# Gated two-branch decode attention on one core: the gate's inputs loaded as three rows and transposed on TensorE, a branch's normalisation on VectorE behind the next unit's scores

## The chip, the core and the metric

The kernel runs on one core of one Trainium2 chip. The core has five engines with instruction queues of their own: TensorE (PE in the profile; its weight loads are PEld), VectorE (DVE), ScalarE (ACT), GpSimd (POOL) and SyncE (SP), which here only issues transfers. An engine works through its own queue in order, and waits at an instruction until the semaphores that it names are there. Transfers between the chip's main memory and the core's buffers run on 16 DMA engines. The metric is the device time of one execution in microseconds (us), lower is better.

## The reference

Two attention branches A and B are computed on the same two tokens `x` (2 x 512) and mixed by a gate. Each branch has its own projection `wq`, its own cached keys and values (2 batches, 32 heads, 4096 positions, 128 numbers each) and its own output projection `wo`. Everything is float32.

```
g = sigmoid((x * gate_w).sum(-1, keepdims=True))
q = (x @ wq)  as 32 heads of 128
p = softmax(q . k_cache * 128 ** -0.5)         # over 4096 positions, for each batch and head
o = p @ v_cache                                # then heads side by side, @ wo
result = g * branch_A + (1 - g) * branch_B     # 2 x 512
```

The caches make nearly all of the bytes: 64 loads of 8.39 MB, beside two of `wq` and two of `wo` of the same size.

## The kernel before

**Units.** The work is cut into 32 units: branch (A, B), batch b (0, 1) and a group g of four heads (0 to 7), in that order, so that units 0 to 15 are branch A and 8, 16 and 24 are the first units of a new batch or branch. `per_branch` is 16, `NU` is 32. A unit loads the keys of four heads as `kt` (128 partitions x 16384 numbers; a partition is one head's run of 128 positions) and the values as `vt` in the same shape.

**One unit.** `scores(u)` multiplies `kt` by the query, which lies in PSUM, in place on VectorE (L147), and sums over the 128 numbers of a head (L149). `soft(u)` takes the maximum on VectorE (L154, L156, L158) and the exponentials on ScalarE (L162, four of them, which also write the sums of the exponentials to `lsum`). `values(u)` multiplies by the values on TensorE (L174). After each second unit ScalarE brings the result to SBUF (L179) and TensorE adds up the four strips into `gat` (L183).

**The end of a batch.** With the last group of a batch `values` calls `outputs(n, b)`: ScalarE copies `gat` (L189), TensorE sums `lsum` over the partitions (L191), VectorE takes the reciprocal of that sum and multiplies it by the gate (L193, L194), TensorE picks each head's row out of `gat` (L197), and ScalarE copies the rows to `rows` with the scale `rl` (L200). With the second batch TensorE also deals the rows out to 128 partitions (L204) and VectorE copies that to `on` (L207). The VectorE instructions L193, L194 and L207 stand in VectorE's queue ahead of the next unit's L147.

**Buffers and the order of the loads.** SyncE issues all large loads in the order in which the program is written, and each waits there until its buffer is free:

- `kt` has two buffers, which are taken in turn by `wq` of A, keys 0, keys 1, and so on; `wq` of B takes one between keys 15 and keys 16, and at the end values 31 and `wo` of B take one each. Keys u+2 can be issued when `scores(u)` has ended. Keys 1 come after `project("A")`, since it reads the buffer that holds `wq` of A (L61).
- `vt` has one buffer. Values u+1 can be issued when `values(u)` has ended (L68). `wo` of A comes last in it.

**The start.** `wq` of A and keys 0 are issued at once by SyncE. The two rows of `x` and `gate_w` are issued by ScalarE as three loads into `xg` (L85 to L88), each of them 128 partitions x 4 numbers, 16 bytes a partition. From `xg` VectorE makes `xb` (L112, the scaled `x`, each number 32 times), `xw` and `zp` (L114, L116); TensorE sums the gate's logit (L119); `project("A")` multiplies `xb` by `wq` on TensorE (L136), 64 matmuls in the program and 128 records in the trace.

**The end.** `bulk` takes the first parts of the output projections on TensorE (L237), a tail of `wo` of B comes in small pieces (L82, L247), and `res` is copied (L250) and stored.

The lines of the program that set the order:

```
    project("A")
    load_k(1)
    load_v(0)
    for u in range(NU):
        scores(u)
        soft(u)
        ...
            load_k(u + 2 if u != per_branch - 1 else per_branch)
        ...
        values(u)
        ...
            load_v(u + 1)
```

Of the kernel before, what the change touches and what calls it, by code (L numbers as in the profile page):

```python
# [8 lines left out]
F32 = mybir.dt.float32  # L9
AF = mybir.ActivationFunctionType  # L10
ALU = mybir.AluOpType
AX = mybir.AxisListType

P = 128
B = 2
H = 32
SK = 4096
DH = 128
D = 512
KC = D // P  # L20
QP = 32
HU = P // QP
SLOTS = SK // QP
VC = 4
# [4 lines left out]
NJ = D * H * DH // (P * D)  # L29
# [8 lines left out]
def tile_gated_decode(ctx: ExitStack, tc: tile.TileContext, ins: dict, out: bass.AP):  # L38
    nc = tc.nc
# [3 lines left out]
    consts = ctx.enter_context(tc.tile_pool(name="consts", bufs=1))  # L43
    work = ctx.enter_context(tc.tile_pool(name="work", bufs=2))
    ps = ctx.enter_context(tc.tile_pool(name="ps", bufs=1, space=bass.MemoryType.PSUM))
# [4 lines left out]
    per_branch = B * HG  # L50
# [31 lines left out]
                nc.sync.dma_start(wo[n][:, i:j], src[:, i:j])  # L82

    load_wq("A")
    xg = consts.tile([P, B + 1, KC], F32)  # L85
    for b in range(B):
        nc.scalar.dma_start(xg[:, b], ins["A_x"][b, 0].rearrange("(p c) -> p c", c=KC))
    nc.scalar.dma_start(xg[:, B], ins["gate_w"].rearrange("(p c) -> p c", c=KC))  # L88
    load_k(0)

    ident = consts.tile([P, P], F32)
    make_identity(nc, ident)
    ones = consts.tile([P, QP], F32)
# [4 lines left out]
    lsum = consts.tile([P, H], F32)  # L98
# [4 lines left out]
    pick = consts.tile([P, VC, H], F32)  # L103
# [3 lines left out]
    deal = consts.tile([H, P + HU], F32)  # L107
    nc.vector.memset(deal, 0.0)
    nc.vector.tensor_copy(deal[:, HU - 1:HU - 1 + P:HU], ident[:H, :H])

    xb = consts.tile([P, B, KC, QP], F32)
    nc.vector.tensor_scalar(xb, xg[:, :B, :, None].to_broadcast([P, B, KC, QP]), SCALE, None, op0=ALU.mult)  # L112
    xw = consts.tile([P, B, KC], F32)
# [6 lines left out]
    gate = consts.tile([H, 4, B], F32)  # L120
# [20 lines left out]
    sc, vp, on = {}, {}, {}  # L141
    gat, rows = {}, {}
# [8 lines left out]
    def soft(u):  # L151
        n, b, g = units[u]
        rm = work.tile([P, QP], F32, name="rm")
        nc.vector.tensor_reduce(rm[:, 0:1], sc[u], axis=AX.X, op=ALU.max)  # L154
        tm = work.tile([P, QP], F32, name="tm")
        nc.vector.transpose(tm, rm[:, 0:1].to_broadcast([P, QP]))  # L156
        nm = work.tile([P, 1], F32, name="nm")
        nc.vector.tensor_reduce(nm, tm, axis=AX.X, op=ALU.max, negate=True)  # L158
        for h in range(HU):
            r = slice(h * QP, (h + 1) * QP)  # L160
            w = pr[r, :, HU:HU + QP].rearrange("p c (a h) -> p c a h", h=HP)[:, :, :, h]
            nc.scalar.activation(w, sc[u][r].rearrange("p (c a) -> p c a", a=VC), AF.Exp, bias=nm[r],  # L162
                                 accum_out=lsum[r, g * HU + h:g * HU + h + 1])
# [23 lines left out]
    def outputs(n, b):  # L187
        gs = work.tile([P, VC, DH], F32, name="vs", bufs=1)
        nc.scalar.activation(gs, gat[n, b].rearrange("p (a d) -> p a d", a=VC), AF.Copy)  # L189
        lt = ps.tile([H, 1], F32, name="small")  # L190
        nc.tensor.matmul(lt, lsum, ones[:, 0:1], start=True, stop=True)  # L191
        rl = work.tile([H, 2], F32, name="rl")
        nc.vector.reciprocal(rl[:, 0:1], lt)  # L193
        nc.vector.tensor_tensor(rl[:, 1:2], rl[:, 0:1], gate[:, 2 + (n == "B"), b:b + 1], op=ALU.mult)  # L194
        o = ps.tile([H, DH], F32, name="small")
        for a in range(VC):
            nc.tensor.matmul(o, pick[:, a], gs[:, a], start=a == 0, stop=a == VC - 1)  # L197
        if b == 0:
            rows[n] = work.tile([H, B, DH], F32, name="rows", bufs=1)
        nc.scalar.activation(rows[n][:, b], o, AF.Copy, scale=rl[:, 1:2])  # L200
        if b == B - 1:
            t = ps.tile([P, B, NJ], F32, name="small")
            for q in range(HU):
                nc.tensor.matmul(t, deal[:, HU - 1 - q:HU - 1 - q + P], rows[n][:, :, q * NJ:(q + 1) * NJ],  # L204
                                 start=q == 0, stop=q == HU - 1)
            on[n] = work.tile([P, NJ, B], F32, name="on")
            nc.vector.tensor_copy(on[n].rearrange("p j b -> p b j"), t)  # L207

    project("A")
    load_k(1)  # L210
# [1 line left out]
    for u in range(NU):  # L212
        scores(u)
        soft(u)
        if u == per_branch - 2:
            load_wq("B")
        elif u == NU - 2:
            load_v(NU - 1)
        elif u == NU - 1:
            load_wo("B")  # L220
        else:
            load_k(u + 2 if u != per_branch - 1 else per_branch)
            if u == per_branch - 1:
                project("B")
                load_k(per_branch + 1)
        values(u)
        if u == NU - 2:
            load_wo("A")
        elif u < NU - 2:
            load_v(u + 1)  # L230

    bulk = ps.tile([P, D], F32, name="q", bufs=4)
    nc.vector.memset(bulk, 0.0)
    for n in "AB":
        for j in range(NJ if n == "A" else NB):
            s = j % STRIPS
            nc.tensor.matmul(bulk[s * QP:s * QP + B], on[n][:, j], wo[n][:, j],  # L237
                             start=n == "A" and j < STRIPS, stop=n == "B" and j >= NB - STRIPS)
# [6 lines left out]
    for j in range(NB, NJ):  # L245
        for s in range(STRIPS):
            nc.tensor.matmul(acc[s * QP:s * QP + B], on["B"][:, j], wo["B"][:, j, s * DH:(s + 1) * DH],  # L247
                             start=False, stop=j == NJ - 1)
# [28 lines left out]
```

## Time and profile before

| what | value |
|---|---|
| time, median of 3 runs | 1368.32 us (1367.85 to 1368.99) |
| time of the profiled execution | 1366.86 us |
| its span, from the first to the last instruction | 1365.1 us |
| VectorE busy | 1127.3 us, 83% of the span |
| TensorE busy (matmuls) | 358.5 us, 26% |
| ScalarE busy | 82.1 us, 6% |
| read from main memory | 570.43 MB, 418 GB/s over the span |

The profiled execution took 1.76 us more than its span, and 1.46 us less than the median of the runs. The profile's times are microseconds from the span's start. A row of the timeline gives the start, the duration, the engine (SPq and ACTq are the queues of SyncE and ScalarE, in which a transfer is issued), the line of the program, the operation, and in square brackets how long the engine had been idle before it and what ended that. A row of the stretches (a window) gives busy times by engine, then the granted TensorE clock, the DMA engines' share and the GB/s; packets count there where they began. A row of the waits gives the total, the number of waits and the longest one.

### The profile page before, as it was taken

How to read it: one execution, taken by the hardware profiler on the slowest of the kernel's cores; microseconds unless marked ns; L12 is line 12 of the kernel's file. 1: busy time of each engine (PE TensorE's matmuls, PEld its weight loads, DVE VectorE, ACT ScalarE, POOL GpSimd, SP SyncE). 2: the span in 40 equal slices, each digit the busy share in tenths (PEclk: the TensorE clock that was granted, in tenths of full speed). 3: DMA queues.
4: the chain of work that ended last, by engine and by line, in shares of the span. 5: the costliest groups of instructions: out<-in, count | busy, mean ns of one | idle time of the engine just before them, and what ended most of it. 6: DMA issues, size and time to landing. Idle time of an engine off the chain costs nothing.

```text
span 1365.1 us, 5925 instructions
## 1 busy us (share of the span) xinstructions
PE 358.5 (26%) x2578; PEld 100.0 (7%) x2578; DVE 1127.3 (83%) x184; ACT 82.1 (6%) x283; POOL 1.8 (0%) x8
## 2 busy tenths in 40 slices
PE   0401222222122222112540222323212222111256
PEld 0100000000000000000110000000000000000011
DVE  0699888998279999998619999999827999999860
ACT  0000000000000000000000000000000000000000
POOL 0000000000000000000000000000000000000000
PEclk9956666665566665566785666665556666566668
DMA  9499999999997999999999999999999799999998
GB/s 411 204 430 430 431 430 431 430 437 444 434 408 307 442 444 433 430 430 431 434 431 436 433 436 431 430 436 438 433 430 432 306 430 429 430 434 431 444 438 349
DMA packets 10986, 570.82 MB, mean 418 GB/s; under 512 B 1608, under 2 KB 1616, under 8 KB 2000
## 3 DMA queue, kind: packets, MB, share of 16 engines
q1 hardware_dynamic: 10520, 570.43, 96.8%
q8 instruction: 20, 0.33, 0.1%
q10 hardware_dynamic: 440, 0.01, 0.0%
q14 instruction: 6, 0.05, 0.0%
HBM read 570.43 MB, written 0.00 MB: 418 GB/s over the span
## 4 chain that ended last, share of the span: by engine, by line
DMA 57%; DVE 21%; PE 17%; another core or an unknown queue 3%; issue 0%; ACT 0%; SPq 0%; ACTq 0%; DVEq 0%
DMA vt<-in_A_v_cache_dram 33%; PE vp L174 16%; DMA vt<-in_B_v_cache_dram 15%; DVE sc L149 10%; DVE kt L147 10%; DMA xg<-in_A_x_dram 3%; DMA kt<-in_B_wo_dram 3%; DMA kt<-in_B_k_cache_dram 3%; PE q L136 1%; PE gat L183 0%; ACT pr L162 0%; DVE rm L154 0%; ACT vs L179 0%; SPq L82 0%
## 5 line engine op out<-in xcount | busy, mean ns | idle before, releaser
L147 DVE TENSOR_TENSOR kt<-kt,q 128x16384 f32<-128x16384 f32 x32 | 550.9, 17215 | 43.1 <-DMA kt<-in_A_k_cache_dram 23.0
L149 DVE TENSOR_REDUCE sc<-kt 128x128 f32<-128x16384 f32 x32 | 551.0, 17220 | 3.2
L174 PE MATMUL vp<-vt,pr 128*32 128x512 f32 x1984 | 278.6, 725 | 916.3 <-DMA vt<-in_A_v_cache_dram 422.8
L174 PEld LDWEIGHTS vp<-vt,pr 128*32 128x32 f32 x1984 | 76.6, 130 | 1116.4 <-issue 1043.5
L162 ACT ACTIVATE pr<-sc,nm 32x128 f32<-32x128 f32 x128 | 66.4, 519 | 837.8 <-DVE nm L158 835.1
L193 DVE RECIPROCAL rl<-small 32x1 f32<-32x1 f32 x4 | 0.6, 156 | 113.2 <-PE gat L183 113.2
L136 PE MATMUL q<-kt,xb 128*32 128x512 f32 x256 | 31.3, 650 | 10.8 <-DMA kt<-in_B_wq_dram 10.8
L112 DVE TENSOR_SCALAR xb<-xg 128x256 f32<-128x256 f32 x1 | 0.3, 294 | 39.6 <-DMA xg<-in_A_x_dram 39.6
L179 ACT ACTIVATE vs<-vp 128x512 f32<-128x512 f32 x16 | 9.6, 597 | 365.0 <-PE vp L174 365.0
L162 ACT ACTIVATION_READ_ACCUMULATOR pr<-sc,nm 32x1 f32 x128 | 25.4, 198 | 0.0
L250 DVE COPY res<-q 128x128 f32<-128x128 f32 x1 | 0.3, 291 | 24.7 <-PE q L247 24.7
L183 PE MATMUL gat<-vs,strip 128*32 128x512 f32 x32 | 16.7, 604 | 11.4 <-ACT vs L179 11.4
L136 PEld LDWEIGHTS q<-kt,xb 128*32 128x32 f32 x256 | 9.5, 119 | 31.7 <-issue 20.0
L119 PE MATMUL small<-zp,ones 128*32 128x2 f32 x2 | 0.3, 204 | 42.8 <-DVE zp L116 42.8
L174 PE MATMUL vp<-kt,pr 128*32 128x512 f32 x64 | 8.4, 684 | 9.9 <-DMA kt<-in_B_v_cache_dram 9.9
L237 PE MATMUL q<-vt,on 128*2 128x512 f32 x64 | 8.9, 721 | 5.9 <-DMA vt<-in_A_wo_dram 5.9
L154 DVE TENSOR_REDUCE rm<-sc 128x1 f32<-128x128 f32 x32 | 9.2, 286 | 1.1
L156 DVE STREAM_TRANSPOSE tm<-rm 128x32 f32<-128x32 f32 x32 | 6.8, 211 | 1.1
L158 DVE TENSOR_REDUCE nm<-tm 128x1 f32<-128x32 f32 x32 | 6.0, 186 | 1.1
L237 PE MATMUL q<-kt,on 128*2 128x512 f32 x48 | 5.5, 592 | 1.9 <-DMA kt<-in_B_wo_dram 1.9
L207 DVE COPY on<-small 128x64 f32<-128x64 f32 x2 | 0.5, 225 | 6.0 <-PE small L204 6.0
L197 PE MATMUL small<-vs,pick 128*32 128x128 f32 x32 | 4.2, 276 | 2.7 <-ACT vs L189 2.7
(40 smaller groups left out, 32.2 us busy)
## 6 DMA issues: line engine op xcount, KB each, us to landing
kt<-in_B_wo_dram SPq DMA_DIRECT2D x1, 4096.0 KB
kt<-in_B_wo_dram SPq DMA_DIRECT2D x1, 2048.0 KB
kt<-in_B_wo_dram SPq DMA_DIRECT2D x1, 1024.0 KB, 39.6
kt<-in_B_wo_dram SPq DMA_DIRECT2D x1, 512.0 KB, 40.3
kt<-in_B_wo_dram SPq DMA_DIRECT2D x2, 256.0 KB, 40.5
kt<-in_A_k_cache_dram SPq DMA_DIRECT2D x16, 40.9
vt<-in_A_v_cache_dram SPq DMA_DIRECT2D x16, 29.5
kt<-in_B_k_cache_dram SPq DMA_DIRECT2D x16, 32.2
```

The source lines that it names most:

```text
L136: nc.tensor.matmul(q[h * QP:(h + 1) * QP], xb[:, b, c, :], cols[:, c, h, half * HG // 2:(half + 1) * HG // 2, :], start=c == 0, stop=c == ...
L147: nc.vector.tensor_tensor(kt[u], kt[u], q[:, None, :].to_broadcast([P, SLOTS, DH]), op=ALU.mult)
L149: nc.vector.tensor_reduce(sc[u], kt[u], axis=AX.X, op=ALU.add)
L154: nc.vector.tensor_reduce(rm[:, 0:1], sc[u], axis=AX.X, op=ALU.max)
L156: nc.vector.transpose(tm, rm[:, 0:1].to_broadcast([P, QP]))
L158: nc.vector.tensor_reduce(nm, tm, axis=AX.X, op=ALU.max, negate=True)
L162: nc.scalar.activation(w, sc[u][r].rearrange("p (c a) -> p c a", a=VC), AF.Exp, bias=nm[r], accum_out=lsum[r, g * HU + h:g * HU + h + 1])
L174: nc.tensor.matmul(o[s * QP:(s + 1) * QP], pr[:, c, at:at + QP], vt[u][:, c * VC:(c + 1) * VC, :].rearrange("p a d -> p (a d)"), start=not ...
L179: nc.scalar.activation(vs, o, AF.Copy)
L183: nc.tensor.matmul(gat[n, b][r:r + QP], strip, vs, start=True, stop=True)
L197: nc.tensor.matmul(o, pick[:, a], gs[:, a], start=a == 0, stop=a == VC - 1)
L237: nc.tensor.matmul(bulk[s * QP:s * QP + B], on[n][:, j], wo[n][:, j], start=n == "A" and j < STRIPS, stop=n == "B" and j >= NB - STRIPS)
```

## The change

Three things are changed.

1. `x` and `gate_w` are loaded by two transfers into `raw`, three partitions of 512 numbers each (2048 bytes a row). Four transposes on TensorE turn them into `xt` (128 partitions x 4 x 3, PSUM), and a VectorE copy makes `xg` as it was.
2. In `outputs` the sum of `lsum` goes into a last column of the tile `o`, beside the picked rows, and ScalarE copies rows and sum together, without a scale. `outputs` has no VectorE instruction any more.
3. The normalisation is a function of its own, `finish(n)`: the reciprocal and the gate for both batches at once, a VectorE multiplication of the rows, then the deal on TensorE and the copy to `on`. `finish("A")` is written behind `scores(16)` and `soft(16)`, `finish("B")` behind the last unit.

```diff
     load_wq("A")
-    xg = consts.tile([P, B + 1, KC], F32)
-    for b in range(B):
-        nc.scalar.dma_start(xg[:, b], ins["A_x"][b, 0].rearrange("(p c) -> p c", c=KC))
-    nc.scalar.dma_start(xg[:, B], ins["gate_w"].rearrange("(p c) -> p c", c=KC))
+    raw = consts.tile([B + 1, D], F32)
+    nc.scalar.dma_start(raw[:B], ins["A_x"].rearrange("b s e -> (b s) e"))
+    nc.scalar.dma_start(raw[B:], ins["gate_w"].rearrange("(o e) -> o e", o=1))
     load_k(0)
...
+    xt = ps.tile([P, KC, B + 1], F32, name="small")
+    for c in range(KC):
+        nc.tensor.transpose(xt[:, c], raw.rearrange("r (p c) -> r c p", c=KC)[:, c], ident[:B + 1, :B + 1])
+    xg = consts.tile([P, B + 1, KC], F32)
+    nc.vector.tensor_copy(xg, xt.rearrange("p c r -> p r c"))
     xb = consts.tile([P, B, KC, QP], F32)
...
-        lt = ps.tile([H, 1], F32, name="small")
-        nc.tensor.matmul(lt, lsum, ones[:, 0:1], start=True, stop=True)
-        rl = work.tile([H, 2], F32, name="rl")
-        nc.vector.reciprocal(rl[:, 0:1], lt)
-        nc.vector.tensor_tensor(rl[:, 1:2], rl[:, 0:1], gate[:, 2 + (n == "B"), b:b + 1], op=ALU.mult)
-        o = ps.tile([H, DH], F32, name="small")
+        o = ps.tile([H, DH + 1], F32, name="small")
+        nc.tensor.matmul(o[:, DH:], lsum, ones[:, 0:1], start=True, stop=True)
         for a in range(VC):
-            nc.tensor.matmul(o, pick[:, a], gs[:, a], start=a == 0, stop=a == VC - 1)
+            nc.tensor.matmul(o[:, :DH], pick[:, a], gs[:, a], start=a == 0, stop=a == VC - 1)
         if b == 0:
-            rows[n] = work.tile([H, B, DH], F32, name="rows", bufs=1)
-        nc.scalar.activation(rows[n][:, b], o, AF.Copy, scale=rl[:, 1:2])
-        if b == B - 1:
-            t = ps.tile([P, B, NJ], F32, name="small")
-            for q in range(HU):
-                nc.tensor.matmul(t, deal[:, HU - 1 - q:HU - 1 - q + P], rows[n][:, :, q * NJ:(q + 1) * NJ],
-                                 start=q == 0, stop=q == HU - 1)
-            on[n] = work.tile([P, NJ, B], F32, name="on")
-            nc.vector.tensor_copy(on[n].rearrange("p j b -> p b j"), t)
+            rows[n] = work.tile([H, B, DH + 1], F32, name="rows", bufs=1)
+        nc.scalar.activation(rows[n][:, b], o, AF.Copy)
+
+    def finish(n):
+        rl = work.tile([H, 2, B], F32, name="rl")
+        nc.vector.reciprocal(rl[:, 0], rows[n][:, :, DH])
+        nc.vector.tensor_tensor(rl[:, 1], rl[:, 0], gate[:, 2 + (n == "B")], op=ALU.mult)
+        r = rows[n][:, :, :DH]
+        nc.vector.tensor_tensor(r, r, rl[:, 1, :, None].to_broadcast([H, B, DH]), op=ALU.mult)
+        t = ps.tile([P, B, NJ], F32, name="small")
+        for q in range(HU):
+            nc.tensor.matmul(t, deal[:, HU - 1 - q:HU - 1 - q + P], r[:, :, q * NJ:(q + 1) * NJ],
+                             start=q == 0, stop=q == HU - 1)
+        on[n] = work.tile([P, NJ, B], F32, name="on")
+        nc.vector.tensor_copy(on[n].rearrange("p j b -> p b j"), t)
...
         scores(u)
         soft(u)
+        if u == per_branch:
+            finish("A")
...
+    finish("B")
     bulk = ps.tile([P, D], F32, name="q", bufs=4)
```

The orders below are of one engine each; behind the change the same lines of the program have other numbers (L147 is L151, L149 is L153, L154 to L158 are L158 to L162).

VectorE around the border of units 7 and 8, before: the last maxima of unit 7, the reciprocal and the gate of batch 0 (`rl`), then the scores of unit 8.

```order
L154 TENSOR_REDUCE rm<-sc 128x1
L156 STREAM_TRANSPOSE tm<-rm 128x32
L158 TENSOR_REDUCE nm<-tm 128x1
L193 RECIPROCAL rl<-small 32x1
L194 TENSOR_TENSOR rl<-rl,gate 32x1
L147 TENSOR_TENSOR kt<-kt,q 128x16384
L149 TENSOR_REDUCE sc<-kt 128x128
```

The same place with the change:

```order
L158 TENSOR_REDUCE rm<-sc 128x1
L160 STREAM_TRANSPOSE tm<-rm 128x32
L162 TENSOR_REDUCE nm<-tm 128x1
L151 TENSOR_TENSOR kt<-kt,q 128x16384
L153 TENSOR_REDUCE sc<-kt 128x128
```

The two instructions on `rl` have gone; the scores of unit 8 stand directly behind unit 7. The border of units 23 and 24 reads alike.

VectorE around the border of branches A and B, before: the end of unit 15, then the end of branch A (`rl` and `on`), then unit 16.

```order
L158 TENSOR_REDUCE nm<-tm 128x1
L193 RECIPROCAL rl<-small 32x1
L194 TENSOR_TENSOR rl<-rl,gate 32x1
L207 COPY on<-small 128x2x32
L147 TENSOR_TENSOR kt<-kt,q 128x16384
L149 TENSOR_REDUCE sc<-kt 128x128
```

With the change, from the scores of unit 16 to those of unit 17:

```order
L151 TENSOR_TENSOR kt<-kt,q 128x16384
L153 TENSOR_REDUCE sc<-kt 128x128
L158 TENSOR_REDUCE rm<-sc 128x1
L160 STREAM_TRANSPOSE tm<-rm 128x32
L162 TENSOR_REDUCE nm<-tm 128x1
L204 RECIPROCAL rl<-rows 32x2
L205 TENSOR_TENSOR rl<-rl,gate 32x2
L207 TENSOR_TENSOR rows<-rows,rl 32x2x128
L213 COPY on<-small 128x2x32
L151 TENSOR_TENSOR kt<-kt,q 128x16384
```

The end of branch A is now four instructions for both batches, a whole unit later on VectorE, between units 16 and 17.

## The prediction

> **What bounds the kernel now.** I read the page first, then the DMA traffic by stretches, then the chain of waits.
>
> ```profile
> span 1365.1 us, 5925 instructions
> GB/s 411 204 430 430 431 430 431 430 437 444 434 408 307 442 444 433 430 430 431 434 431 436 433 436 431 430 436 438 433 430 432 306 430 429 430 434 431 444 438 349
> q1 hardware_dynamic: 10520, 570.43, 96.8%
> q10 hardware_dynamic: 440, 0.01, 0.0%
> ```
>
> 570.43 MB are 68 loads of 8.39 MB. The traffic stands at 430 to 444 GB/s in nearly all slices, with three holes, in slices 2, 13 and 32. The stretches show them:
>
> ```profile
> 40.00:42.00 2.00, 0.00 (x0) 0.00 (x0) 0.00 (x0) 0.00 (x0) 0.00 (x0) 1.00 0.05 1
> 42.00:59.00 17.00, 15.39 (x130) 5.38 (x130) 11.97 (x7) 0.16 (x1) 0.00 (x0) 1.00 0.00 1
> 59.00:372.00 313.00, 66.77 (x458) 17.95 (x462) 269.95 (x40) 18.41 (x67) 0.00 (x0) 0.61 1.00 432
> 408.00:418.00 10.00, 0.00 (x0) 0.00 (x0) 10.00 (x1) 0.00 (x0) 0.00 (x0) 0.50 0.00 0
> 1058.00:1067.00 9.00, 0.00 (x0) 0.00 (x0) 9.00 (x1) 0.00 (x0) 0.00 (x0) 0.50 0.00 0
> ```
>
> From 59 to 372 us the DMA engines are full at 432 GB/s; in the holes they move nothing. So DMA bounds the kernel, and what can be won is the time in which no load is queued. The values' arrival in a full stretch gives its price (in the chain TensorE starts on them 0.14 us after they land):
>
> ```profile
> 99.67 9.12 PE vp L174 x64
> ...
> 371.93 9.52 PE vp L174 x64
> ...
> 459.21 8.55 PE vp L174 x64
> ...
> 692.65 7.11 PE vp L174 x64
> ...
> 750.49 9.68 PE vp L174 x64
> 789.66 8.87 PE vp L174 x64
> ...
> 1022.19 8.66 PE vp L174 x64
> ```
>
> And from the timeline, behind the third hole:
>
> ```profile
> 1110.07 9.05 PE L174 MATMUL vp<-vt,pr 128*32 128x512 f32 x64 [31.21 <-DMA vt<-in_B_v_cache_dram]
> 1303.66 9.53 PE L174 MATMUL vp<-vt,pr 128*32 128x512 f32 x64 [28.47 <-DMA vt<-in_B_v_cache_dram]
> ```
>
> These are values 0, 7, 9, 15, 16, 17, 23, 25 and 30. A unit (two loads) takes 272.26/7 = 38.89, 233.44/6 = 38.91, 271.70/7 = 38.81 and 193.59/5 = 38.72 us; over all 25 units 38.84, so 19.42 a load.
>
> **Part 1, the start: three rows and a transpose.** The chain, the waits of SyncE's queue and the landing of `xg`'s loads:
>
> ```profile
> 1.19 40.94 DMA xg<-in_A_x_dram
> ...
> 43.06 15.24 PE q L136 x125
> ...
> 58.32 0.33 SPq L61
> ```
>
> ```profile
> SPq L61 <- PE q L136: 51.6, 2, 35.7
> SPq L61 <- DMA kt<-in_A_wq_dram: 21.0, 1, 21.0
> ```
>
> ```profile
> DMA to landing us min/median/max: 22.0/40.6/40.9
> ```
>
> ```profile
> 1.67 0.45 ACTq L88 DMA_DIRECT2D xg<-in_gate_w_dram  x1
> ```
>
> SyncE waits 35.7 us for the projection, to 58.3; so `wq` of A had landed at 58.3 - 35.7 = 22.6. The projection could not start then, because `x` came only at 1.19 + 40.94 = 42.13, when keys 0 were done too (22.6 + 19.4 = 42.0). The landings of 22.0 and 40.6 look like turn-taking: 440 packets on that queue are three loads of 128 pieces and 16 completions and a few for the output, so 9 packets on each of 16 engines per load, and a large load likewise is 8 pieces and a completion. One small packet for one large one makes the first row land with `wq`, the second with keys 0: as seen. A turn is 22.0/9 = 2.4 us.
>
> With the change each of the two loads is at most a piece and a completion per engine if a row is one run, or 16 even pieces: two turns each, four in all, 9.8 us after an issue near 1.2, so about 11 us. What comes then (before: 43.06 - 42.13 = 0.93 us from `x` to the projection) grows by four transposes and a copy, at 0.3 us each 1.5 us, and all of it is hidden under the wait for `wq` to 22.6, with 9 us to spare. Bounds: nothing, or, if the rows land only with `wq` as the first row did, 2.5 us later.
>
> The projection then runs from 22.6 + 0.1 to 37.9 at 15.24 us. Keys 1 and values 0 are issued there. An issue into an empty queue costs 99.53 - 58.32 - 38.84 = 2.4 us above the two loads, so it must come before 42.0 - 2.4 = 39.6: 1.7 us are left. Then the queue never runs dry, and values 0 land at 22.6 + 3 x 19.42 = 80.9 and not 99.53. **Gain 18.6 us.**
>
> How sure the 15.24 us are, the second projection shows:
>
> ```profile
> 673.20 15.90 PE L136 MATMUL q<-kt,xb 128*32 128x512 f32 x128 [10.80 <-DMA kt<-in_B_wq_dram]
> ```
>
> ```profile
> 674.00:676.00 2.00, 2.00 (x16) 0.58 (x12) 0.00 (x0) 0.00 (x0) 0.00 (x0) 0.50 0.91 393
> ```
>
> It started at a granted clock of 0.50 and took 15.90, while the first ran at 1.00 throughout (the stretch 42 to 59). With 15.90 the issue comes at 38.6, still 1.0 before the limit. The Trainium skill, "TensorE: Matmul & The Clock Gate", section "Part 1: The HAM clock gate", says that an idle TensorE stands at half clock, and that only some 3.4 us of steady work lift it. By that rule the new projection would start at half clock after 22 us of idleness; the trace agrees at the second projection (0.50), and not at the first, where the clock is 1.00 after 42 idle us. By either one the sum is the same and the margin 1.7 or 1.0 us.
>
> What is next late: keys 2. Unit 0's scores start when keys 0 land, 42.0 (48.02 in the order of before), and a unit's scores take 34.57 us:
>
> ```profile
> 711.79 17.22 DVE L147 TENSOR_TENSOR kt<-kt,q 128x16384 f32<-128x16384 f32 x1 [6.62 <-DMA kt<-in_B_k_cache_dram]
> ```
>
> ```profile
> 746.36 0.33 SPq L61 DMA_DIRECT2D kt<-in_B_k_cache_dram  x1
> ...
> 781.60 0.33 SPq L61 DMA_DIRECT2D kt<-in_B_k_cache_dram  x1
> ```
>
> 746.36 - 711.79 = 34.57, and 781.60 - 746.36 = 35.24 for a whole unit on VectorE. So keys 2 are issued at 76.6; the limit is 80.9 - 2.4 = 78.5. That is 1.9 us of margin, and it grows by 38.84 - 35.24 = 3.6 a unit.
>
> **Part 2, units 8 and 24: no VectorE work at a batch's end.**
>
> ```profile
> 383.25 0.15 DVE L193 RECIPROCAL rl<-small 32x1 f32<-32x1 f32 x1 [33.99 <-PE gat L183]
> ```
>
> ```profile
> 348.50 0.33 SPq L61 DMA_DIRECT2D kt<-in_A_k_cache_dram  x1
> 381.46 0.33 SPq L68 DMA_DIRECT2D vt<-in_A_v_cache_dram  x1
> 418.06 0.33 SPq L61 DMA_DIRECT2D kt<-in_A_k_cache_dram  x1
> ```
>
> VectorE stood 33.99 us at the reciprocal, until values 7 had been worked off; unit 8's scores therefore ended at 418.06 and keys 10 were issued only there. The two loads issued at 348.50 and 381.46 were in by 371.8 + 38.84 = 410.6, and the queue was empty. With the change nothing of the batch's end stands on VectorE: unit 8's scores start when keys 8 are there, as in any other unit, and keys 10 are issued some 30 us earlier, long before the limit. The sum of `lsum` stays on TensorE and the copy on ScalarE with one column more (nothing: both engines wait for values 8 afterwards). The holes cost 459.21 - 371.93 - 2 x 38.84 = 9.6 us and 1110.07 - 1022.19 - 77.68 = 10.2 us. **Gain 19.8 us.** The scale on ScalarE goes at no cost either way.
>
> **Part 3, `finish("A")` behind unit 16.** It adds four instructions to VectorE between units 16 and 17, and within them a wait for TensorE. Nearest rows:
>
> ```profile
> 703.67 1.23 PE L204 MATMUL small<-rows,deal 32*128 32x64 f32 x8 [0.45 <-ACT rows L200]
> 704.94 0.22 DVE L207 COPY on<-small 128x64 f32<-128x64 f32 x1 [3.05 <-PE small L204]
> ```
>
> ```profile
> L112 DVE TENSOR_SCALAR xb<-xg 128x256 f32<-128x256 f32 x1 | 0.3, 294 | 39.6 <-DMA xg<-in_A_x_dram 39.6
> ```
>
> 0.15 + 0.15 (as L193) + 0.3 (256 numbers a partition, as L112) + 1.23 + 0.22 and some 0.3 of hand-overs are 2.4 us; bounds 0.8 (the VectorE work alone) and 4. `rows` has been ready since about 703, TensorE is idle until values 16 at 750.4, and unit 16's exponentials are queued ahead, so nobody else is late. Behind it wait unit 17's scores and with them keys 19, issued at 781.60 + 2.4 = 784.0; values 17 land at 789.5, so the limit is 787.1. Cost: nothing, with 3.1 us of cover; beyond that each us counts in full. Keys 18 (746.36, ahead of it, limit 750.35 - 2.4 = 747.9) don't move. What stood here before costs nothing today: unit 16 waited for its keys anyway (6.62 us).
>
> **Part 4, `finish("B")` at the end.**
>
> ```profile
> 1336.51 0.23 DVE L207 COPY on<-small 128x64 f32<-128x64 f32 x1 [2.92 <-PE small L204]
> ...
> 1342.34 8.94 PE L237 MATMUL q<-vt,on 128*2 128x512 f32 x64 [5.87 <-DMA vt<-in_A_wo_dram]
> ```
>
> The reciprocal, which ran beside TensorE's work, and the new multiplication come in a row: `on` is ready about 0.7 us later, 1337.5, with two memsets of 512 and 128 numbers a partition behind it, at L112's rate under 1 us together. `wo` of A lands at 1342.2, so almost 4 us of cover hide it; the last piece of `wo` of B sets the end as before.
>
> **The sum.** 18.6 + 9.6 + 10.2 = 38.4 us: 1366.86 - 38.4 = 1328.5 for an execution like the profiled one. Counted forward: `wq` at 22.6, 67 more loads at 19.42 are 1301.1, so 1323.7; behind the last landing
>
> ```profile
> 1361.73 0.45 PE q L247 x8
> ```
>
> 1365.1 - 1361.7 = 3.4 to the span's end and 1.76 outside the span: 1328.9. The median lies 1.46 above the profiled execution, so I say 1330. With the extremes of the load time, 67 x 19.36 and 67 x 19.455, it is 1326 to 1332.5; without the 1.46, 1324.5 at the low end.
>
> **The rivals.**
>
> *The start's hole stays in part or whole.* The margins are 1.7 (keys 1) and 1.9 us (keys 2). If `x` lands only with `wq` the projection ends at 40.4 and some 1 to 3 us of hole stay: 1331 to 1333. If the rows still came with keys 0, all of it: 1330 + 18.6 = 1348.6. For it: the queue is the same one, beside the same large loads. Against: the turn-taking above.
>
> *A hole at 8 or 24 stays, because another wait takes the place of L193's.* VectorE's next one could be for ScalarE, which must have read the scores of two units earlier; but that was done when unit 6's values were. Each that stays is 10 us: 1340, or 1350 for both.
>
> *Slower.* The three rows become many small pieces on one or two engines, one turn each. The decision point is a landing later than 42.1 + 19.8 = 61.9 us, where the start loses what part 2 wins. With 4-byte pieces on one engine 1024 of them would wait; 18 go by 42.0, and the rest, at the pace of the 9 that the gate's row had left when keys 0 ended (issued at 1.67, landed by 42.3, so 0.03 us each), end near 72: the start is 30 us later than today, 1330 + 18.6 + 30 = 1379. Against it: 384 of 440 packets were runs of four numbers each, so a packet was a run and not a number. The Trainium skill, "DMA: Bandwidth & Descriptors", section "Rules for kernel authors", speaks against such a load too: an outermost dimension under 16 confines a transfer to at most that many engines. No run here shows yet how the rows are spread.
>
> **How the numbers follow.** All three holes close: 0.84, 1330. The start's hole stays in part or whole: 0.08. One or both of the others stay: 0.05. No change within 0.2% (2.7 us, about what a measurement of this kernel can tell from no change): 0.01, as gains and losses would have to cancel. Slower: 0.02. Faster sums to 0.97. The range goes from 1324 to 1340: the load time's bounds, the start's margins, and one hole of 10 us.
>
> **What the profile would show.** Right: `raw` lands before 15 us; the projection starts near 22.7 and ends near 38; keys 1 are issued before 39.6; TensorE takes up values 0 near 81; no slice between the first and the last under 425 GB/s; VectorE starts unit 8 on keys 8; `finish("A")` holds VectorE 2 to 3 us. Wrong: a slice 2 near 204 or 300 GB/s; a slice near 307 in the middle; values' distances of 40 us or more in full stretches, which would mean that the load time itself has grown.

## The result, and the profile after

The changed kernel takes 1329.51 us (median of 6 runs, 1328.7 to 1329.98) against 1368.4 us (6 runs, 1367.53 to 1368.99): ratio 0.9716, 95% interval 0.9704 to 0.9729. That is 38.9 us less; the forecast was 1330 with a range of 1324 to 1340. The profiled execution took 1329.9 us with a span of 1328.1.

From its page: the span, the traffic in 40 slices, the queue that ScalarE issues, and the shares of the chain.

```profile
span 1328.1 us, 5928 instructions
GB/s 411 441 416 433 442 434 425 436 439 431 433 434 438 431 433 432 437 434 434 429 438 417 424 438 431 427 439 436 435 428 436 437 434 429 434 437 434 430 433 331
q10 hardware_dynamic: 14, 0.01, 0.0%
DVE 58%; DMA 41%; issue 0%; PE 0%; SPq 0%; DVEq 0%
```

The three holes of 204, 307 and 306 GB/s have gone; but for the first and the last slice nothing lies under 416. Three slices (416, 417 and 424) lie a little under the 425 that the prediction named; the one of 417 holds a small hole, of which more below. The queue of the small loads has 14 packets and not 440. More than half of the chain is now VectorE, which looks like a new bound; e8 below shows that it isn't one.

The start in the timeline:

```profile
1.19 37.36 SPq L61 DMA_DIRECT2D kt<-in_A_k_cache_dram  x2
10.40 0.61 PE L112 MATMUL small<-ident,raw 3*128 3x3 f32 x4 [10.40 <-DMA raw<-in_gate_w_dram]
22.74 15.41 PE L140 MATMUL q<-kt,xb 128*32 128x512 f32 x128 [10.54 <-DMA kt<-in_A_wq_dram]
38.60 0.43 SPq L68 DMA_DIRECT2D vt<-in_A_v_cache_dram  x1
43.41 17.22 DVE L151 TENSOR_TENSOR kt<-kt,q 128x16384 f32<-128x16384 f32 x1 [30.45 <-DMA kt<-in_A_k_cache_dram]
```

The transposes run at 10.40, the projection waits for `wq` and nothing else, and the second load of the first row, keys 1, has been issued by 38.55; before it was 58.64. TensorE then takes up values 0, 7, 9, 23 and 25 at these times:

```profile
82.40 9.43 PE L178 MATMUL vp<-vt,pr 128*32 128x512 f32 x64 [44.25 <-DMA vt<-in_A_v_cache_dram]
...
354.18 8.37 PE L178 MATMUL vp<-vt,pr 128*32 128x512 f32 x64 [29.70 <-DMA vt<-in_A_v_cache_dram]
...
431.45 8.99 PE L178 MATMUL vp<-vt,pr 128*32 128x512 f32 x64 [29.09 <-DMA vt<-in_A_v_cache_dram]
...
993.95 9.34 PE L178 MATMUL vp<-vt,pr 128*32 128x512 f32 x64 [28.75 <-DMA vt<-in_B_v_cache_dram]
...
1072.21 9.46 PE L178 MATMUL vp<-vt,pr 128*32 128x512 f32 x64 [30.85 <-DMA vt<-in_B_v_cache_dram]
```

Against before, values 0 come 17.3 us earlier, the stretch from values 7 to 9 is 77.27 and not 87.28 us (10.0 less), that from 23 to 25 is 78.26 and not 87.88 (9.6 less): 36.9 in all. Unit 8 on VectorE, and the issue of keys 10 at its end:

```profile
334.75 17.22 DVE L151 TENSOR_TENSOR kt<-kt,q 128x16384 f32<-128x16384 f32 x1 [3.25 <-DMA kt<-in_A_k_cache_dram]
...
369.32 0.33 SPq L61 DMA_DIRECT2D kt<-in_A_k_cache_dram  x1
```

VectorE waits 3.25 us for its keys, as it does in the units beside it (3.3 to 3.4 at units 7 and 9), and no longer 33.99 for TensorE. The border of the branches, with `finish("A")`:

```profile
684.11 17.22 DVE L151 TENSOR_TENSOR kt<-kt,q 128x16384 f32<-128x16384 f32 x1 [43.51 <-DMA kt<-in_B_k_cache_dram]
...
719.36 0.14 DVE L204 RECIPROCAL rl<-rows 32x2 f32<-32x2 f32 x1
719.53 0.15 DVE L205 TENSOR_TENSOR rl<-rl,gate 32x2 f32<-32x2 f32 x1
719.72 0.41 DVE L207 TENSOR_TENSOR rows<-rows,rl 32x256 f32<-32x256 f32 x1
722.25 0.22 DVE L213 COPY on<-small 128x64 f32<-128x64 f32 x1 [2.12 <-PE small L210]
722.39 17.21 DVE L151 TENSOR_TENSOR kt<-kt,q 128x16384 f32<-128x16384 f32 x1
```

From 719.36 to 722.39 it holds VectorE for 3.0 us. At the end:

```profile
1300.55 0.22 DVE L213 COPY on<-small 128x64 f32<-128x64 f32 x1 [1.95 <-PE small L210]
...
1304.46 9.36 PE L246 MATMUL q<-vt,on 128*2 128x512 f32 x64 [3.96 <-DMA vt<-in_A_wo_dram]
```

`on` is there at 1300.8, 3.5 us before `wo` of A.

### The profile page after: what moved, and what is told of

Read it like the earlier page. It is cut to its first block, busy times and chain, and to the rows that moved or that the text cites. A ratio compares the mean times of both kernels' runs of the same rounds, so it can differ in the third digit from the quotient of the medians.

```text
span 1328.1 us, 5928 instructions
## 1 busy us (share of the span) xinstructions
PE 365.5 (28%) x2582; PEld 102.9 (8%) x2582; DVE 1128.2 (85%) x183; ACT 81.6 (6%) x283; POOL 1.8 (0%) x8
## 4 chain that ended last, share of the span: by engine, by line
DVE 58%; DMA 41%; issue 0%; PE 0%; SPq 0%; DVEq 0%
DVE sc L153 29%; DVE kt L151 28%; DMA kt<-in_A_k_cache_dram 19%; DMA kt<-in_B_k_cache_dram 19%; DMA kt<-in_B_wo_dram 3%; DVE rm L158 0%; DVE tm L160 0%; PE small L210 0%; DVE nm L162 0%; SPq L82 0%; PE q L256 0%; DVE rows L207 0%; SPq L72 0%; DVEq L153 0%; DVE res L259 0%
## 5 line engine op out<-in xcount | busy, mean ns | idle before, releaser
L151 DVE TENSOR_TENSOR kt<-kt,q 128x16384 f32<-128x16384 f32 x32 | 551.0, 17218 | 135.8 <-DMA kt<-in_B_k_cache_dram 72.9
L153 DVE TENSOR_REDUCE sc<-kt 128x128 f32<-128x16384 f32 x32 | 551.0, 17220 | 3.1
L178 PE MATMUL vp<-vt,pr 128*32 128x512 f32 x1984 | 281.6, 731 | 849.9 <-DMA vt<-in_A_v_cache_dram 448.9
L140 PE MATMUL q<-kt,xb 128*32 128x512 f32 x256 | 32.3, 668 | 20.6 <-DMA kt<-in_A_wq_dram 10.5
L259 DVE COPY res<-q 128x128 f32<-128x128 f32 x1 | 0.3, 292 | 22.7 <-PE q L256 22.7
L210 PE MATMUL small<-rows,deal 32*128 32x64 f32 x16 | 3.7, 405 | 44.8 <-DVE rows L207 44.8
L140 PEld LDWEIGHTS q<-kt,xb 128*32 128x32 f32 x256 | 8.8, 121 | 43.3 <-issue 32.7
L158 DVE TENSOR_REDUCE rm<-sc 128x1 f32<-128x128 f32 x32 | 9.2, 286 | 1.1
L162 DVE TENSOR_REDUCE nm<-tm 128x1 f32<-128x32 f32 x32 | 6.0, 186 | 1.1
L210 PEld LDWEIGHTS small<-rows,deal 32*128 32x128 f32 x16 | 3.4, 309 | 45.3 <-ACT pr L166 43.8
```

What stands on the lines that cost most here:

```text
L140: nc.tensor.matmul(q[h * QP:(h + 1) * QP], xb[:, b, c, :], cols[:, c, h, half * HG // 2:(half + 1) * HG // 2, :], start=c == 0, stop=c == ...
L151: nc.vector.tensor_tensor(kt[u], kt[u], q[:, None, :].to_broadcast([P, SLOTS, DH]), op=ALU.mult)
L153: nc.vector.tensor_reduce(sc[u], kt[u], axis=AX.X, op=ALU.add)
L178: nc.tensor.matmul(o[s * QP:(s + 1) * QP], pr[:, c, at:at + QP], vt[u][:, c * VC:(c + 1) * VC, :].rearrange("p a d -> p (a d)"), start=not ...
L210: nc.tensor.matmul(t, deal[:, HU - 1 - q:HU - 1 - q + P], r[:, :, q * NJ:(q + 1) * NJ], start=q == 0, stop=q == HU - 1)
```

## The experiments

The theory: the time is that of 68 full loads plus the time in which no large load is queued; the change closes three such holes, and all else is covered. Each kernel was run beside the kernel before; the first four, the next four and the last three each on one chip. The edits are against the changed kernel unless said otherwise.

| run | median, us | ratio to before (95%) |
|---|---|---|
| e1_rows_only | 1349.17 | 0.9859 (0.9844 to 0.9874) |
| e2_finish_only | 1348.89 | 0.9860 (0.9845 to 0.9875) |
| e3_x_ahead | 1329.63 | 0.9718 (0.9703 to 0.9732) |
| e4_row_pieces | 1350.61 | 0.9873 (0.9856 to 0.9889) |
| e5_half_proj | 1328.51 | 0.9712 (0.9696 to 0.9728) |
| e6_finish_early | 1329.16 | 0.9717 (0.9703 to 0.9732) |
| e7_long_finish | 1338.77 | 0.9785 (0.9771 to 0.9800) |
| e8_half_mult | 1327.84 | 0.9705 (0.9691 to 0.9720) |
| e9_split_wq | 1328.83 | 0.9713 (0.9699 to 0.9727) |
| e10_wait_at_8 | 1340.33 | 0.9799 (0.9785 to 0.9813) |
| e11_change | 1329.42 | 0.9718 (0.9704 to 0.9732) |

**The parts alone.** e1 is the kernel before with the three-row load, its transposes and the copy, and the old end of a batch. e2 is the changed kernel with the old loads:

```diff
-    raw = consts.tile([B + 1, D], F32)
-    nc.scalar.dma_start(raw[:B], ins["A_x"].rearrange("b s e -> (b s) e"))
-    nc.scalar.dma_start(raw[B:], ins["gate_w"].rearrange("(o e) -> o e", o=1))
+    xg = consts.tile([P, B + 1, KC], F32)
+    for b in range(B):
+        nc.scalar.dma_start(xg[:, b], ins["A_x"][b, 0].rearrange("(p c) -> p c", c=KC))
+    nc.scalar.dma_start(xg[:, B], ins["gate_w"].rearrange("(p c) -> p c", c=KC))
...
-    xt = ps.tile([P, KC, B + 1], F32, name="small")
...
```

> The three-row load and the transposes alone, with the batch's end as before. Theory (what counts is only the time in which no large load is queued): the start's hole closes and the holes at units 8 and 24 stay, 17.3 us less than before (values 0 at 82.3 and not 99.5), so 1351. Rival (VectorE's total work is what bounds, since 58% of the changed kernel's chain is VectorE): VectorE starts only 4.6 us earlier (43.4 and not 48.0), so 1364.

> The normalisation behind the next unit's scores alone, with x and the gate's weights loaded as before. Theory: slice 2 stays at about 204 GB/s, the holes at 8 and 24 close, 19.6 to 20.6 us less than before, so 1348. Rival (the holes share a cause: with the start closed the queue has less slack, and closing one alone gives more or less than its share): both parts alone sum to something else than the 38.9 us of the whole change by more than 2 us.

The traffic of e1, then of e2:

```profile
GB/s 405 432 436 432 436 436 434 436 432 434 429 304 436 434 434 432 429 420 436 437 436 432 436 432 433 434 434 436 436 436 358 345 434 437 436 436 431 436 434 352
```

```profile
GB/s 405 187 436 436 434 436 428 430 427 430 436 436 436 436 436 432 434 430 434 434 436 426 422 434 436 434 434 436 436 436 436 434 434 432 428 436 432 436 432 318
```

e1 closes the hole in slice 2 and keeps the two in the middle (304; 358 and 345, which is one hole across two slices). e2 does the opposite. The parts win 19.0 and 19.2 us; their sum of 38.2 is the whole change's 38.9 within what a run can tell, so the holes add up and neither part needs the other. The rival for e1 (VectorE's 4.6 us earlier start and no more) falls, and so does that for e2: the sums differ by 0.7 us and not by more than 2. e1 won 1.7 us more than the 17.3 that I had expected, e2 0.4 less than the lower end of its 19.6 to 20.6.

**Why x was late: turns.** e3 undoes the rows and moves the three old loads to SyncE, ahead of `wq`; e4 keeps the rows and cuts each into 16 pieces.

```diff
+    xg = consts.tile([P, B + 1, KC], F32)
+    for b in range(B):
+        nc.sync.dma_start(xg[:, b], ins["A_x"][b, 0].rearrange("(p c) -> p c", c=KC))
+    nc.sync.dma_start(xg[:, B], ins["gate_w"].rearrange("(p c) -> p c", c=KC))
     load_wq("A")
...
```

```diff
-    nc.scalar.dma_start(raw[:B], ins["A_x"].rearrange("b s e -> (b s) e"))
-    nc.scalar.dma_start(raw[B:], ins["gate_w"].rearrange("(o e) -> o e", o=1))
+    stage = big.tile([P, SLOTS, DH], F32, name="vt", bufs=1)
+    nc.scalar.dma_start(stage[:B, :16, :D // 16], ins["A_x"].rearrange("b s (j i) -> (b s) j i", j=16))
+    nc.scalar.dma_start(stage[B:B + 1, :16, :D // 16], ins["gate_w"].rearrange("(o j i) -> o j i", o=1, j=16))
...
+    nc.vector.tensor_copy(raw.rearrange("r (j i) -> r j i", j=16), stage[:B + 1, :16, :D // 16])
```

> The change with x and the gate's weights loaded as before (384 pieces of 16 bytes, no transposes), but issued by SyncE ahead of wq. Theory (x was late because its pieces took turns with the large loads' pieces, one for one): ahead of the large loads the pieces don't wait, x lands before 6 us, wq is issued 1.3 us later, the projection starts with wq at 24 and the time is 1330 to 1331. Rival (384 pieces of 16 bytes are slow by themselves): x lands near 40 again and the time is 1346 to 1349.

> The change with two loads of the three rows, each row cut into 16 pieces of 128 bytes (48 pieces in all, through a staging buffer with one more VectorE copy of about 0.6 us). Theory (turns): the first DMA engine has at least 19 small packets against 18 large ones, so x lands only when keys 0 have, at 42 to 44 us, the start's hole is back, and the time is 1346 to 1350. Rival (the number or smallness of the pieces): 48 pieces are an eighth of the 384 of before, x lands within 12 us and the time is that of the change, 1329 to 1331.

The first user of `x` in e3's timeline, and its projection:

```profile
2.96 0.29 DVE L112 TENSOR_SCALAR xb<-xg 128x256 f32<-128x256 f32 x1 [0.30 <-DMA xg<-in_A_x_dram]
...
24.11 16.75 PE L136 MATMUL q<-kt,xb 128*32 128x512 f32 x128 [20.08 <-DMA kt<-in_A_wq_dram]
```

The first user in e4's, its loads of keys on SyncE, and from its page the small loads' queue:

```profile
1.19 60.95 SPq L61 DMA_DIRECT2D kt<-in_A_k_cache_dram  x2
...
43.01 0.41 DVE L111 COPY raw<-vt 3x512 f32<-3x512 f32 x1 [40.35 <-DMA vt<-in_gate_w_dram]
```

```profile
q10 hardware_dynamic: 74, 0.01, 0.0%
```

384 pieces of 16 bytes land before 2.96 us when they stand ahead of the large loads; 48 pieces of 128 bytes land at 43.0 when they take turns with them. The turns themselves stand in the traces, which keep the start and the length of every DMA packet. Before, 16 pieces of 16 bytes (one for each DMA engine) begin between 4.90 and 5.30 us, the next 16 between 7.32 and 7.72, and so on every 2.42 us, which is the length of one 64 KB packet of the large loads; the last 144 go together at 41.3 to 41.7, when keys 0 are through. So neither the number nor the size of the pieces made `x` late, but the turns, and the transposes are one way to be rid of them: e3 without them takes 1329.63. e3 lies 0.4 under what the theory gave it; e4 lies at 1350.61, 0.6 above its upper end, with the start's hole back (keys 1 issued by 62.1).

The packet counts agree. 8 packets of that queue are the output's (e3 has only these). The change adds 6: two rows and two completions, one row and one completion. e4 adds 66: 32 pieces of `x` with 2 completions, and 16 pieces with 16. The Trainium skill, "DMA: Bandwidth & Descriptors", section "Why a DMA increments its semaphore by 16 and not by 1", says that the slowest dimension sets the number of engines, and that each of these adds a completion; the counts fit that with 2 engines for the two rows, 2 and 16 for the pieces, and 1 for the row of `gate_w`, which went as one run. Its section "Queues, rings and completion order" says that an engine goes round between the queues packet by packet; the packets every 2.42 us bear that out, with one small packet a turn.

**The middle: the wait, not the work.** e10 puts one unused VectorE instruction back, at the end of branch A's first batch alone:

```diff
+        if n == "A" and b == 0:
+            nc.vector.reciprocal(work.tile([H, 1], F32, name="idle"), o[:, DH:])
```

> The change with one unused reciprocal of 32 numbers on VectorE put back at the end of branch A's first batch, where it waits for TensorE's sum. Theory (the wait itself makes the hole, whatever the instruction is worth): VectorE stands some 34 us ahead of unit 8, slice 12 falls to 300 to 410 GB/s, unit 24 stays without a hole, and the time is 9.6 to 10 us over the change's, 1339. Rival (the holes came from the longer chain at a batch's end, with the scale on ScalarE): under 1 us more.

> The change itself again, beside the other two on the same chip: 1329 to 1330 by every theory.

In e10's timeline, and its slices:

```profile
366.04 0.16 DVE L199 RECIPROCAL idle<-small 32x1 f32<-32x1 f32 x1 [34.90 <-PE small L197]
...
400.66 0.33 SPq L61 DMA_DIRECT2D kt<-in_A_k_cache_dram  x1
```

```profile
GB/s 408 439 417 430 437 439 435 431 433 433 432 284 439 437 433 421 433 433 439 437 435 421 437 435 426 437 433 433 437 437 431 432 435 432 433 437 435 437 432 336
```

An instruction of 0.16 us costs 10.9 us (1340.33 against 1329.42 for e11, measured beside it): VectorE stands 34.90 us before it, keys 10 are issued at 400.66 instead of 369.32, and slice 12 falls to 284. That is a little more than the 9.6 to 10 expected, and a slice below the 300 to 410 expected; the other borders stay full. By the packets of e10's trace a DMA engine stands idle there for 10.9 us on average, which is what the run lost. The rival with the longer chain falls.

**The border of the branches.** e6 writes `finish("A")` ahead of the scores of unit 16; e7 leaves it behind them and adds work.

```diff
+        if u == per_branch:
+            finish("A")
         scores(u)
         soft(u)
-        if u == per_branch:
-            finish("A")
```

```diff
         nc.vector.tensor_copy(on[n].rearrange("p j b -> p b j"), t)
+        if n == "A":
+            scratch = consts.tile([P, QP], F32)
+            for _ in range(26):
+                nc.vector.tensor_reduce(scratch, ident.rearrange("p (s q) -> p q s", q=QP), axis=AX.X, op=ALU.add)
```

> The change with finish(A) written ahead of the scores of unit 16 and not behind them, so that VectorE waits for TensorE's end of unit 15 before unit 16's scores. Theory (at this border VectorE waits for its keys anyway, which land at 684 while unit 15's rows are there at 677): no difference, 1329 to 1330. Rival (any VectorE wait for the end of a batch costs a hole, as at units 8 and 24): about 10 us more, 1339.

> The change with 26 more reductions on VectorE at the end of finish(A), some 9.6 us in all. Theory (a load must be issued 2.4 us before the queue runs dry; keys 19 were issued at 756.9, values 17 landed at 761.4, so 2.1 us of cover are left): a hole of 7.5 us behind values 17 and as much more time, 1337. Rival (VectorE's 3.4 us of idle time a unit takes the work up, a single delay costs nothing): 1329.5.

Unit 16's first instruction in e6 comes at the same time as in the change, behind a wait for keys:

```profile
683.99 17.22 DVE L151 TENSOR_TENSOR kt<-kt,q 128x16384 f32<-128x16384 f32 x1 [3.80 <-DMA kt<-in_B_k_cache_dram]
```

So the position at this border makes no difference (1329.16). In e7 the added work and the next issue, and a stretch of its traffic:

```profile
721.42 10.67 DVE L217 TENSOR_REDUCE scratch<-ident 128x32 f32<-128x128 f32 x26
...
766.50 0.33 SPq L61 DMA_DIRECT2D kt<-in_B_k_cache_dram  x1
```

```profile
758.00:760.00 2.00, 0.00 (x0) 0.00 (x0) 2.00 (x1) 0.00 (x0) 0.00 (x0) 0.50 0.08 33
760.00:762.00 2.00, 0.00 (x0) 0.00 (x0) 2.00 (x1) 0.00 (x0) 0.00 (x0) 0.50 0.00 0
```

The work was 10.7 us and not 9.6, and the time is 9.6 over e6's on the same chip. With the 2.1 us of cover that I had counted it would have been 10.7 - 2.1 = 8.6. So the delay does count in full beyond its cover, and the rival (idle time takes it up) falls; but the cover was nearer to 1 us than to 2: the limit lies about a us earlier than "2.4 us before the last landing". The packets show why. The 16 DMA engines don't end together: in e7 thirteen of them end their last packet ahead of the hole between 757.9 and 758.6, the other three at 759.5, 760.3 and 760.6, and a load has landed only with the last. Keys 19's packets begin at 767.5 to 768.2, so an engine stands idle for 9.0 us on average.

The same count finds a small hole in the change itself. Keys 18 are issued at 718.68, which is before the limit by landings, yet the engines run out one by one from 717.8, and stand idle for 0.9 us on average. It is 0.5 us in e6 and 0.4 in e11.

**Is VectorE the new bound?** e8 multiplies only the first half of the positions.

```diff
-        nc.vector.tensor_tensor(kt[u], kt[u], q[:, None, :].to_broadcast([P, SLOTS, DH]), op=ALU.mult)
+        half = kt[u][:, :SLOTS // 2]
+        nc.vector.tensor_tensor(half, half, q[:, None, :].to_broadcast([P, SLOTS // 2, DH]), op=ALU.mult)
```

> The change with half of the multiplication of the keys by the query left out in every unit, so that VectorE needs 26.6 and not 35.2 us a unit. Theory (DMA bounds, VectorE is only an early link of the chain): 1328 to 1330. Rival (VectorE bounds, 58% of the chain is VectorE): up to 8.6 us a unit less, 1055 at the end and anything under 1320 as a part of that.

From its page:

```profile
PE 365.2 (28%) x2582; PEld 103.3 (8%) x2582; DVE 856.0 (65%) x183; ACT 81.5 (6%) x283; POOL 1.8 (0%) x8
DMA 74%; PE 22%; DVE 2%; another core or an unknown queue 1%; issue 0%; SPq 0%; DVEq 0%
```

272 us of VectorE's work less leave 1327.84, some 1.5 us less (0.2 under what the theory gave it). The chain passes to DMA and TensorE while the time hardly moves: in the change it ran through VectorE because keys are issued when VectorE frees their buffer, though the queue had loads in it nearly all the while. With the shorter multiplications keys 18 are issued at 708.16, and the hole of 0.9 us there is gone; that can be a good part of what e8 gains.

**The 1.3 us at the start.** Values 0 came at 82.3 and not at the forecast 80.9. e5 leaves half of branch A's projection out; e9 does the whole of it, but in two halves with `wq` loaded in two.

```diff
-                for c in range(KC):
+                nk = KC // 2 if n == "A" else KC
+                for c in range(nk):
...
-                            start=c == 0, stop=c == KC - 1)
+                            start=c == 0, stop=c == nk - 1)
```

```diff
+        src = ins[n + "_wq"].rearrange("(p c) f -> p c f", c=KC)
+        for c in range(0, KC, 2) if n == "A" else [0]:
+            e = c + 2 if n == "A" else KC
+            nc.sync.dma_start(wq[n][:, c:e], src[:, c:e])
...
+        parts = [range(0, 2), range(2, KC)] if n == "A" else [range(KC)]
+        for part, b, half in [(k, b, f) for k in parts for b in range(B) for f in range(2)]:
...
```

> The change with half of branch A's projection left out (the contraction over two of four parts), so that keys 1 are issued near 30.5 and not 38.5. It asks where the 1.3 us went by which values 0 landed later (82.3) than forecast (80.9). Theory (the issue at 38.5 is early enough, the 1.3 us are the spread of the 16 DMA engines' landings): values 0 land at 82 to 82.6 again and the time is 1329 to 1330. Rival (the margin of 1.7 us was too small and engines that were done with keys 0 stood idle): values 0 land near 81 and the time is 1328 to 1328.5.

> The change with wq of A loaded in two halves and the projection done half by half, the first half while the second one loads, so that keys 1 are issued near 31 without leaving work out. Theory (as the half projection showed, values 0 land 1.6 us earlier when keys 1 are queued before 33): keys 0 land at 42, values 0 at 80.7 to 81, and the time is 0.5 to 1.5 us under the change's. Rival (the half projection gained by its smaller work on TensorE and not by the earlier issue): values 0 at 82.3 and the change's time.

Unit 0's first multiplication, which waits for keys 0, and values 0 in e5:

```profile
42.05 17.22 DVE L152 TENSOR_TENSOR kt<-kt,q 128x16384 f32<-128x16384 f32 x1 [29.10 <-DMA kt<-in_A_k_cache_dram]
...
80.81 9.88 PE L179 MATMUL vp<-vt,pr 128*32 128x512 f32 x64 [48.20 <-DMA vt<-in_A_v_cache_dram]
```

The transposes, the two halves of the projection, the issue behind it, the first multiplication and values 0 in e9:

```profile
7.70 0.61 PE L115 MATMUL small<-ident,raw 3*128 3x3 f32 x4 [7.70 <-DMA raw<-in_gate_w_dram]
...
12.95 8.78 PE L144 MATMUL q<-kt,xb 128*32 128x512 f32 x64 [3.46 <-DMA kt<-in_A_wq_dram]
22.59 7.08 PE L144 MATMUL q<-kt,xb 128*32 128x512 f32 x64 [0.86 <-DMA kt<-in_A_wq_dram]
30.09 0.43 SPq L68 DMA_DIRECT2D vt<-in_A_v_cache_dram  x1
...
43.07 17.22 DVE L155 TENSOR_TENSOR kt<-kt,q 128x16384 f32<-128x16384 f32 x1 [32.81 <-DMA kt<-in_A_k_cache_dram]
...
81.72 8.53 PE L182 MATMUL vp<-vt,pr 128*32 128x512 f32 x64 [52.05 <-DMA vt<-in_A_v_cache_dram]
```

e5 spoke for the rival of its own expectation: values 0 at 80.7, and 1328.51. e9 was to confirm that with all the work done, and did not: keys 1 are issued even earlier, but values 0 land at 81.6, against 82.3 in the change and 82.0 in e11. Its time, 1328.83 (1328.62 to 1329.46), is not apart from e11's 1329.42 (1328.76 to 1330.57). Nor do the other runs with the change's start and its loads (e1, e6, e7, e8, e10) follow the issue: they issue keys 1 between 38.7 and 40.0 and land values 0 between 81.7 and 82.5 in no order. And e3, where values 0 land at 83.3, is no slower than the change, so a us at this place can't be read off the times.

The packets show where the 1.3 us went. The profile counts 20 packets of 16 KB in a queue of the kind "instruction". In the change one of them begins at 34.22, while keys 0 load, and takes 0.96 us; the next packet on that DMA engine takes 2.88 instead of 2.42. The other 15 engines begin their last packet of keys 0 between 38.5 and 39.3, this one at 40.46, and keys 0 have landed only with it. From 40 to 41 us it shows as traffic that e5 doesn't have: two packets in the change and two in e9, one of them from this engine (the change, e9, e5):

```profile
40.00:41.00 1.00, 0.00 (x0) 0.00 (x0) 0.00 (x0) 0.00 (x0) 0.00 (x0) 1.00 0.31 131
```

```profile
40.00:41.00 1.00, 0.00 (x0) 0.00 (x0) 0.00 (x0) 0.00 (x0) 0.00 (x0) 0.50 0.30 131
```

```profile
40.00:41.00 1.00, 0.00 (x0) 0.00 (x0) 0.00 (x0) 0.00 (x0) 0.00 (x0) 0.50 0.00 0
```

e9 has the packet at 26.59, and e5, with half of the projection's instructions, has none there. In the kernel before it came at 51.55, inside the hole. So neither expectation of e5 holds: the earlier landing in e5 came with its smaller work, as the rival of e9 said, through the instructions that needn't be loaded. No run moves this packet by itself; the reading rests on the traces.

## Why the prediction was right, point by point

*DMA bounds, and holes are what can be won.* Shown: e1, e2 and e10 open and close single holes, each for its price, and e8 takes a quarter of VectorE's work away for 1.5 us. The packets say the same: between the first and the last slice a DMA engine stood idle for 38.0 us on average before, nearly all of it in the three holes, and for 1.0 with the change, and the profiled spans differ by just that, 37.0 us.

*The start.* The rows landed at 10.4 (forecast 11), the projection ran from 22.74 to 38.15 (22.7 to 37.9), keys 1 were issued at 38.5, before the limit of 39.6. The gain was 17.3 us and not 18.6: this term was mis-sized, since keys 0 landed at 43.3 and not at 42.0, and values 0 as much later; the sum had no term for the instruction packet. The mechanism (turns) is shown by e3, e4 and the packets, but the four turns that I counted for the rows were not what happened. The two rows of `x` began at 1.66 us, ahead of the first large packet (1.77), and took no turn; only the row of `gate_w` did, behind two large packets, with a third ahead of its completion (7.43 and 9.92). That 10.4 came so near to 11 is luck.

*TensorE's clock.* Here I read the trace wrongly. I took the clock column's 1.00 at the start as evidence against the Trainium skill, "TensorE: Matmul & The Clock Gate". The number of matmuls in 2 us of the changed kernel's projection says otherwise (the second number with an x is TensorE's weight loads):

```profile
23.00:25.00 2.00, 2.00 (x12) 0.39 (x8) 0.00 (x0) 0.00 (x0) 0.00 (x0) 1.00 1.21 524
25.00:27.00 2.00, 2.00 (x20) 0.56 (x16) 0.00 (x0) 0.00 (x0) 0.00 (x0) 1.00 1.06 459
27.00:29.00 2.00, 2.00 (x24) 0.51 (x20) 0.00 (x0) 0.00 (x0) 0.00 (x0) 1.00 0.30 131
```

About half as many matmuls pass in the first 2 us as later, with 1.00 in the column throughout; the trace's first record of the clock stands only at 25.8 us, when the pace doubles, and the column shows 1.00 ahead of it. In the kernel before it is the same (first record at 45.7), and e9's first half takes 8.78 us, its second 7.08 for as many. So TensorE does start slow behind idleness, as Part 1 of that page of the Trainium skill says, and the column does not show it there. The sum did not hang on it. But the projection took up to 16.9 us (e1), more than the 15.24 and 15.90 that I reckoned with, and there keys 1 were issued at 40.0, past my limit of 39.6, with no loss that the times can show.

*Units 8 and 24.* 19.6 us against 19.8, in the split 10.0 and 9.6 against 9.6 and 10.2.

*`finish("A")`.* 3.0 us against 2.4, within the bounds of 0.8 to 4; the deal on TensorE took 1.93 and not 1.23, at a granted clock of 0.50 after 43.57 us of idleness:

```profile
720.27 1.93 PE L210 MATMUL small<-rows,deal 32*128 32x64 f32 x8 [43.57 <-DVE rows L207]
```

It was covered, as forecast, but with less to spare: I forecast 3.1 us of cover, the change's trace read by my limit gives 2.1, and e7 shows about 1. That is the step with the least behind it: a limit taken from the last landing is late by a us or so. By the same limit keys 18 were to be in time; they were not quite, with 0.9 us of idle engines.

*`finish("B")`.* Hidden, with 3.5 us to spare (almost 4).

*The sum.* The ends of the range from the load time come to 1332.7 and 1324.9 by the terms given, not 1332.5 and 1324.5; nothing hangs on that. The three holes gave 36.9 us in the profiled executions, 1.5 less than the forecast 38.4, and their spans differ by 37.0 (1365.1 to 1328.1). The medians differ by 38.9. What is left between them is the spread of single executions: the profiled one of before was 1.5 us under its median, that of the change 0.4 over its own. My step from the profiled time to the median was thus worth as much as the term that I had mis-sized, and the closeness of 1330 to 1329.51 owes something to that, which is luck.

## What to carry to other kernels

Where the transfers are full nearly everywhere, look for the stretches in which none is queued, and follow each back to what the next issue waited for: here 0.15 us of VectorE behind a wait cost 10 us, and 6 KB of input behind turns cost 17. A tiny load that shares the DMA engines with large ones should have few pieces per engine, or stand ahead of them in the same queue; both did equally well here. An engine with the most of the chain needn't be the bound: take work from it before believing so. And a load has landed when its slowest DMA engine is done, while the others may have run dry long before: issue the next one earlier than the landing suggests.

## What the runs showed of the hardware that was not expected

- A small packet's turn is as long as one packet of the large load. With `wq` in halves, so with packets of 1.21 and not 2.42 us, the row of `gate_w` and its completion began 1.29 us apart and not 2.49, and the rows had landed at 7.7 and not at 10.4 us.
- The granted clock's column read 1.00 from the start of each execution while TensorE began its first projection at about half pace; the first record of the clock came 2.9 to 5.9 us later. Where this projection was done whole, it took 15.2 to 16.9 us for the same matmuls.
- A hole costs what the 16 DMA engines stand idle on average (10.9 us in e10, 9.0 in e7 for 9.6 us of time), and they don't begin to stand together: in e7 the first was done at 757.9 and the last at 760.6.
- Packets of the kind "instruction" take turns on the same DMA engines: the engine that had one of 16 KB among its packets of keys 0 was the last to finish them, and keys 0 landed 1.3 us later than forecast.
